# One list of places for all operations of a packed-attention and SoLU kernel, and low parts of w_out made by products

## The chip, the cores and the metric

The kernel runs on one core of a Trainium2 chip. The metric is the device time of one execution in microseconds (us); the time before is the median of three runs. The profile is one further execution on the same kind of chip.

The engines have short names: PE is TensorE (PEld its weight loads), DVE is VectorE, ACT is ScalarE, POOL is GpSimd, and SP is the engine that issues the DMAs. Each engine takes its instructions in program order; between engines, semaphores make one wait for another. The matrix products go to PSUM banks, which are given out from small pools.

## The reference

```
# q, k, v: (8 batches, 8 heads, 576 rows, 64), p: (8, 8, 32, 64), float32; w_in (512, 1024), w_out (1024, 512)
def sm_attn(qq, kk, vv):
    s = scale * np.matmul(qq, kk.transpose(0, 1, 3, 2))
    s = s - np.max(s, axis=-1, keepdims=True)
    a = np.exp(s)
    a = a / (np.sum(a, axis=-1, keepdims=True) + 1e-09)
    return np.matmul(a, vv)
p_packed = sm_attn(p, k, v)
out = sm_attn(q, p_packed, p_packed)
...
h = x @ w_in                      # x: (4608 tokens, 512), the attention's output
h_max = np.max(h, axis=-1, keepdims=True)
e = np.exp(h - h_max)
sm = e / (np.sum(e, axis=-1, keepdims=True) + 1e-09)
solu = h * sm
mu = np.mean(solu, axis=-1, keepdims=True)
var = np.mean((solu - mu) ** 2, axis=-1, keepdims=True)
ln = (solu - mu) / np.sqrt(var + 1e-06) * g_ln
return (ln @ w_out).astype(np.float32)
```

The two weights arrive as 64-bit floats (8 MB together); the kernel itself turns their words into float32.

## The kernel before, in words

Weights. w_in is loaded in four blocks and w_out in four blocks of 1 MB each. To make float32 of a block takes two steps on ACT (lines 534 and 544: the exponent part, then the last bits; block 0 has its last bits done by DVE, LOW_BY = 'daaaaaaa'), one on DVE that joins them (line 545, the magnitude), two products on PE that sum the columns of magnitudes (line 560 or 620), and one on DVE that sets the sign (line 550, signed). Then w_out is scaled by a power of two and by g_ln and split into a high half-precision part wch (ACT, line 636) and a low one wcl = scaled w_out - wch (DVE, line 637); eight chunks of 128x512, so eight steps each.

Attention of a batch b (names as in the tables of the program): lk, lv, lq load k, v, q; kt and qt turn k and q by 32x32 blocks on DVE (batch 0: by products with the identity on PE and copies on ACT); s10, s11 are the scores of the pack queries on PE, mx the maxima on DVE, ex the exponentials on ACT; tp and tc transpose them (PE, ACT); av is the product with v; pp scales its rows (DVE), pt and pc transpose (PE, DVE), pk, to and un make the batch's power-of-two unit. sx0, sx1 are the scores of the second attention (PE), sb puts them into blocks (DVE), sm, su, se, ss, sn are its softmax (DVE, POOL, ACT, DVE, POOL; in batch 0 su and sn are on DVE). z0, z1 multiply the packed rows by w_in (PE), zh and zl are the high and low halves of that (ACT, DVE; in batch 0 POOL makes three of the four zl from copies by ACT, ZL_BY). at, ah, al turn the second attention's weights and split them (DVE, ACT, POOL).

Token tiles. There are 36 tiles of 128 tokens; batch b has 576 tokens, so tiles 4, 13, 22 and 31 lie half in one batch and half in the next. For a tile: m1 is 12 products of 512 columns (attention weights by z, in a high and a low part; line 1173) into an h bank pair, of which there are two; nm is the row maximum and bd a bound (DVE), ex the exponential (ACT, line 1193), u = e * h (DVE, line 1198), which frees h; mu the mean (POOL); yh and yl the high and low half of u - mu (ACT line 1206, DVE line 1209); tr a transposing DMA; m2a and m2b are 24 products by wch and wcl (PE, line 1232) into the one bank po; sq and cr make the row's factor (ACT, POOL); ev writes the tile from po (ACT, line 1236), st stores it. An h pair is free after u, the po bank after ev.

What sets the order. Batch 0 and the weights are written out by hand, with a priority for each step (tables PACK0, W_IN, UNPACK0, W_OUT, PARTS), and the framework's own scheduler places their instructions. Batches 1 to 7 and the tiles are operations of a plan: each has a due place, for example tile number plus a figure for the step,

```
add(i + where[name], f'{name}-{i}', fn, args, needs, takes, gives)
```

and perform() issues the first in that order whose needs are done and whose buffers are free; manual dependencies keep this order on each engine. Thirteen products of ones by ones (keep_busy, line 581) stand at three places to keep PE at work; their results are not used.

Of the kernel before, what the change touches and what calls it, by code (L numbers as in the profile page):

```python
# [19 lines left out]
A_TOP = 15  # L20
LOW_BY = 'daaaaaaa'
ZL_BY = 'ppdp'
A2L_BY = 'pddd'
B0_BY = 'dddd'
PACK0 = [-5, 395, 2010, 10, -1605, 60, -2910, 200, 195]
W_IN = [-50, -50, 4100, 50]
UNPACK0 = [-50, 350, -95, 0, 0, -25, -20, 0, 280]
W_OUT = [-1050, 0, -1030, 2990]
SCALE_AT = 610
CHUNKS = [4, 2, 1, 7, 5, 6, 0, 3]  # L30
PARTS = [100, -2850, 3000, 0, -2010, -1050, -3750, 200]
AHEAD = 0
NPA = 3
NPO = 1
B1_ROWS = 0
TILE = {'m1': -0.05,
 'nm': 0.519,
 'bd': -2.929,
 'ex': 0.729,
 'u': -4.879,  # L40
 'mu': 0.979,
 'yh': 0.948,
 'yl': 1.201,
 'tr': -3.808,
 'sq': 2.299,
 'cr': 0.617,
 'm2a': 2.36,
 'm2b': 2.62,
 'ev': 2.833,
 'st': 3.924,  # L50
 'busy': 0.088}
ATT = {'lk0': -17.433,
 'lk1': -11.934,
 'lk2': -10.358,
 'lk3': -7.951,
 'lv0': -11.338,
 'lv1': -9.338,
 'lv2': -6.267,
 'lq0': -13.937,
 'lq1': -11.104,  # L60
 'lq2': -10.158,
 'lq3': -6.991,
 'kt0': -6.473,
 'kt1': -11.582,
 'kt2': -40.791,
 'kt3': -12.895,
 's10': -5.478,
 'mx0': -29.228,
 'ex0': -4.953,
 'es0': -6.154,  # L70
 's11': -6.498,
 'mx1': -31.812,
 'ex1': -4.556,
 'es1': -5.662,
 'rs': -10.952,
 'tp0': -37.333,
 'tc0': -16.585,
 'tp1': -23.866,
 'tc1': -5.94,
 'tp2': -45.982,  # L80
 'tc2': -30.812,
 'av': -4.062,
 'pp': -36.699,
 'pt': -3.743,
 'pk': -21.304,
 'pc': -3.628,
 'to': -2.366,
 'un': -14.125,
 'qt0': -5.112,
 'qt1': -4.802,  # L90
 'qt2': -6.292,
 'qt3': -26.802,
 'sx0': -12.059,
 'sb0': -2.809,
 'sx1': -32.569,
 'sb1': -19.701,
 'sm0': -27.009,
 'su0': -32.306,
 'se0': -12.207,
 'ss0': -13.505,  # L100
 'sn0': -15.146,
 'sm1': -2.44,
 'su1': -1.798,
 'se1': -13.119,
 'ss1': -17.879,
 'sn1': -9.579,
 'z0': -2.081,
 'zh0': -14.416,
 'zl0': -10.393,
 'z1': -0.678,  # L110
 'zh1': -0.357,
 'zl1': -0.394,
 'at0': -0.887,
 'ah0': -16.535,
 'al0': -2.069,
 'at1': -0.509,
 'ah1': -26.161,
 'al1': -35.456}
MORE = {1: {'lk0': -17.127,
     'lk1': -10.418,  # L120
     'lk2': -9.443,
     'lk3': -8.697,
     'lv0': -9.318,
     'lv1': -57.431,
     'lv2': -5.306,
     'lq0': -13.393,
     'lq1': -9.739,
     'lq2': -6.037,
     'lq3': -5.441,
     'kt0': -6.813,  # L130
     'kt1': -17.476,
     'kt2': -23.913,
     'kt3': -15.876,
     's10': -6.487,
     'mx0': -40.712,
     'ex0': -13.175,
     'es0': -3.538,
     's11': -5.503,
     'mx1': -25.02,
     'ex1': -16.458,  # L140
     'es1': -36.133,
     'rs': -18.456,
# [36 lines left out]
     'zl1': -22.172,
     'at0': -0.926,  # L180
     'ah0': -10.634,
     'al0': -16.855,
     'at1': -6.048,
     'ah1': -32.66,
     'al1': -27.591},
 '1': {'lk0': -31.677,
       'lk1': -21.074,
       'lk2': -14.417,
       'lk3': -10.52,
       'lv0': -29.172,  # L190
# [60 lines left out]
       'al1': -20.563},
 't0': {'m1': -5.97,
        'nm': -10.524,
        'bd': -4.667,
        'ex': -10.568,
        'u': -16.555,
        'mu': -27.616,
        'yh': -22.199,
        'yl': -27.731,
        'tr': -13.33,  # L260
        'sq': -5.133,
        'cr': -7.345,
# [60 lines left out]
        'yl': -1.729,
        'tr': -1.96,
        'sq': -0.595,
        'cr': 0.135,
        'm2a': 2.872,
        'm2b': -13.057,
        'ev': -18.471,
        'st': 1.764,  # L330
        'busy': -0.291},
 't33': {'m1': 0.331,
         'nm': -1.714,
         'bd': -14.347,
# [24 lines left out]
         'm2a': 11.669,
# [29 lines left out]

# [888 lines left out]
```

## Time and profile before

| | |
|---|---|
| median of three runs | 435.77 us (435.16 to 435.9) |
| the profiled execution | 433.67 us, of which its span on the core is 431.9 us |
| PE busy | 388.8 us, 90% of the span |
| DVE busy | 331.3 us, 77% |
| ACT busy | 247.7 us, 57% |
| POOL busy | 135.3 us, 31% |
| moved by DMA | 66.99 MB, mean 155 GB/s |

The profile's page gives the busy time of each engine, the groups of instructions by line, and the chain of work that ended last. A further view gives busy time by stretches ("windows"); the clock in it is the share of TensorE's full clock that was granted. Matrix products overlap their neighbours, so one that is busy for 0.38 us can follow the one before after 0.22 us. Where rows on DVE or ACT follow back to back, one starts up to 0.1 us before the other's recorded end.

### The profile page before, as it was taken

What the parts mean: (1) busy time and instruction counts of PE and PEld (TensorE: products, weight loads), DVE (VectorE), ACT (ScalarE), POOL (GpSimd) and SP (SyncE); (2) the same over time, 40 slices, a digit from 0 to 9 for tenths busy, and PEclk for the clock granted to TensorE, in tenths of its full rate; (3) what the DMA queues carried; (4) which work ended last, traced back from release to release, by engine and by line L of the source; (5) the groups of instructions that cost most, each with busy time, mean ns of one, the idle gap of its engine ahead of it and who ended that gap; (6) DMA issues with size and microseconds to landing.
All of it is one profiled execution on the core that took longest, in us unless ns stands there. A gap on an engine that the chain in (4) does not pass through costs nothing.

```text
span 431.9 us, 8093 instructions
## 1 busy us (share of the span) xinstructions
PE 388.8 (90%) x3053; PEld 179.5 (42%) x3053; DVE 331.3 (77%) x662; ACT 247.7 (57%) x422; POOL 135.3 (31%) x268
## 2 busy tenths in 40 slices
PE   7697075499999999999999999999999999999985
PEld 6472021243443344344543453345434543444432
DVE  3459997769898878897879897988888969765540
ACT  2687453634563686467546844776376636755641
POOL 0000431106332343434115533441153525421230
PEclk9999668699999999999999999999999999999999
DMA  9999970799898957949787969296645431324372
GB/s 272 354 335 258 231 123 15 145 163 180 162 212 180 174 109 184 169 79 190 166 190 146 200 96 257 49 178 151 163 102 114 118 103 45 103 75 121 74 154 66
DMA packets 243383, 66.99 MB, mean 155 GB/s; under 512 B 216464, under 2 KB 236944, under 8 KB 242832
## 3 DMA queue, kind: packets, MB, share of 16 engines
q1 hardware_dynamic: 243344, 66.47, 69.2%
q8 instruction: 24, 0.39, 0.4%
q14 instruction: 15, 0.12, 0.1%
HBM read 37.23 MB, written 9.44 MB: 108 GB/s over the span
## 4 chain that ended last, share of the span: by engine, by line
PE 75%; DVE 10%; ACT 5%; issue 4%; SPq 3%; DMA 2%; POOL 1%; ACTq 0%; DVEq 0%
PE po L1232 41%; PE h L1173 19%; PE pa L1066 4%; PE pa L991 3%; PE pa L940 2%; PE pa L974 2%; PE pa L1028 2%; DVE u L1198 2%; DMA zh<-in_moe_w_in_dram 2%; SPq L449 1%; ACT yhl L1206 1%; DVE yhl L1209 1%; SPq L441 1%; DVE nm L1177 1%; PE pa L581 1%
## 5 line engine op out<-in xcount | busy, mean ns | idle before, releaser
L1232 PE MATMUL po<-wch,yT 128*128 128x512 f16 x576 | 181.8, 380 | 1.9 <-ACT o_sb L1236 1.9
L1232 PEld LDWEIGHTS <-yT 128*128 128x128 f16 x864 | 81.7, 98 | 112.1 <-issue 19.2
L1232 PE MATMUL po<-wcl,yT 128*128 128x512 f16 x288 | 109.2, 379 | 0.0
L1173 PE MATMUL h<-zh,a2h 128*128 128x512 f16 (+1 forms) x160 | 56.4, 391 | 12.1 <-ACT a2h L835 7.8
L1209 DVE SCALAR_TENSOR_TENSOR yhl<-u,negmu,yhl 128x1024 f16<-128x1024 f32 x36 | 45.6, 1265 | 23.7 <-ACT yhl L1206 23.7
L1193 ACT ACTIVATE e<-h,bias,unit 128x1024 f32<-128x1024 f32 x36 | 43.3, 1202 | 34.8 <-DVE bound L1185 21.5
L1198 DVE SCALAR_TENSOR_TENSOR u<-e,s_row,h 128x1024 f32<-128x1024 f32 x36 | 45.9, 1276 | 16.7 <-ACT e L1193 16.3
L1173 PE MATMUL h<-zh,a2l 128*128 128x512 f16 (+1 forms) x160 | 55.9, 387 | 0.3 <-POOL a2l L836 0.3
L1173 PE MATMUL h<-zl,a2h 128*128 128x512 f16 (+1 forms) x160 | 55.9, 387 | 0.0
L1206 ACT ACTIVATE yhl<-u,negmu 128x1024 f16<-128x1024 f32 x36 | 41.3, 1147 | 19.6 <-POOL negmu L1202 19.2
L1173 PEld LDWEIGHTS <-a2h 128*128 128x128 f16 (+1 forms) x320 | 27.9, 102 | 50.7 <-issue 9.6
L1177 DVE TENSOR_REDUCE nm<-h 128x1 f32<-128x1024 f32 x36 | 43.4, 1206 | 1.6 <-PE h L1173 1.6
L1236 ACT ACTIVATE o_sb<-po,c_row 128x512 f32<-128x512 f32 x36 | 24.6, 682 | 34.2 <-PE po L1232 15.3
L1217 ACT ACTIVATE e<-u,negmu 128x1024 f32<-128x1024 f32 x36 | 41.0, 1138 | 0.0
L1202 POOL TENSOR_SCALAR negmu<-su 128x1 f32<-128x1 f32 x36 | 6.8, 190 | 89.0 <-DVE u L1198 84.9
L1224 POOL TENSOR_SCALAR c_row<-sq,k_out,s_eps 128x1 f32<-128x1 f32 x36 | 15.7, 436 | 47.4 <-ACT e L1217 46.0
L1094 POOL TENSOR_TENSOR a2l<-s,a2h 128x576 f16<-128x576 f32 x14 | 18.8, 1343 | 29.4 <-ACT a2h L1090 29.4
L1042 POOL TENSOR_TENSOR s<-s,mx 128x576 f32<-128x576 f32 x14 | 17.2, 1227 | 26.5 <-DVE mx L1039 26.5
L1055 POOL TENSOR_TENSOR a<-a,sm 128x576 f32<-128x576 f32 x14 | 18.6, 1332 | 19.6 <-DVE sm L1052 19.6
L955 ACT ACTIVATE e<-pa,nmx 128x288 f32<-128x288 f32 x28 | 13.7, 494 | 19.1 <-DVE nmx L947 19.1
L1046 ACT ACTIVATE a<-s 128x576 f32<-128x576 f32 x14 | 9.5, 682 | 24.6 <-POOL s L1042 24.6
L1173 PEld LDWEIGHTS <-a2l 128*128 128x128 f16 (+1 forms) x160 | 14.6, 102 | 18.7 <-issue 1.3
(153 smaller groups left out, 544.5 us busy)
## 6 DMA issues: line engine op xcount, KB each, us to landing
out_dram<-o_sb SPq DMA_DIRECT2D x36, 256.0 KB, 2.9
v_sb<-in_v_dram SPq DMA_DIRECT2D x16, 512.0 KB, 5.2
raw<-in_k_dram SPq DMA_DIRECT2D x28, 288.0 KB, 4.7
raw<-in_q_dram SPq DMA_DIRECT2D x28, 288.0 KB, 3.9
zh<-in_moe_w_in_dram SPq DMA_DIRECT2D x2, 1024.0 KB, 5.8
zl<-in_moe_w_in_dram SPq DMA_DIRECT2D x2, 1024.0 KB, 6.8
raw<-in_moe_w_out_dram SPq DMA_DIRECT2D x2, 1024.0 KB, 7.6
zh<-in_moe_w_out_dram SPq DMA_DIRECT2D x2, 1024.0 KB, 8.1
```

Of the source, the lines that this page charges most:

```text
L1055: nc.gpsimd.tensor_tensor(out=st['a2', r], in0=st['a2', r], in1=st['sm', r].unsqueeze(2).broadcast_to([P, NB, J]), op=ALU.mult)
L1066: nc.tensor.matmul(bank[r][32 * g:32 * g + 32, :], lhsT=st['ppT'][rows, r, 32 * g:32 * g + 32], rhs=w_in_sb[rows, g, 512 * n:512 * n + 512 ...
L1094: nc.gpsimd.tensor_tensor(out=lo, in0=a2T, in1=hi, op=ALU.subtract)
L1173: nc.tensor.matmul(h[rows, 512 * n:512 * n + 512], lhsT=lhsT, rhs=z[:, r, 512 * n:512 * n + 512], start=t == 0, stop=t == end)
L1177: nc.vector.tensor_reduce(out=nm, in_=st['h'], axis=AX.X, op=ALU.max, negate=True)
L1193: nc.scalar.activation(st['e'], st['h'], AF.Exp, bias=st['bias'], scale=st['unit'][:, 1:2], accum_out=st['se'])
L1198: nc.vector.scalar_tensor_tensor(out=st['u'], in0=st['e'], scalar=st['s_row'], in1=st['h'], op0=ALU.mult, op1=ALU.mult, accum_out=st['su'])
L1206: nc.scalar.activation(st['y'][:, 0], st['u'], AF.Identity, bias=st['negmu'])
L1209: nc.vector.scalar_tensor_tensor(out=st['y'][:, 1], in0=st['u'], scalar=st['negmu'], in1=st['y'][:, 0], op0=ALU.add, op1=ALU.subtract)
L1217: nc.scalar.activation(st['e'], st['u'], AF.Square, bias=st['negmu'], accum_out=st['sq'])
L1232: nc.tensor.matmul(st['po'], lhsT=st['yT'][:, a, c], rhs=w[:, c], start=c == 0 and t == 0, stop=c == NFC - 1 and t == 2)
L1236: nc.scalar.activation(st['o'], st['po'], AF.Copy, scale=st['c'])
```

## The change

All operations, the loads and the weights' conversion and batch 0 among them, become operations of the plan, and their places come from one list of some 1,500 names. A name is op/batch, op-tile, or op/w for the weights' preparation: lw0 to lw3 load blocks of w_in and lW0 to lW3 blocks of w_out; for the eight blocks wa and wl are the two steps on ACT, wm the magnitude, wp the column sums, ws the sign; ch, cm and cl concern the eight chunks of wch and wcl; lp, p0, lP, pa, pd, px prepare p.

- The token tiles are listed out of turn: 0, 3, 2, 1, 5, 6, 4, 7, 9, 10, 12, 8, 11, 13 and so on by m1; the tiles across two batches come after whole tiles of their second batch.
- The low part of a chunk of w_out is made on PE: a float32 product of a diagonal matrix of the scale (diag, ACT) and w_out, from which a half-precision product of minus the identity and wch is subtracted in PSUM; ACT casts the bank to wcl. DVE has no wcl step left.
- In batch 0 all four zl and both al are DVE's; POOL has no elementwise step there. All eight blocks take their last bits on ACT.
- The keep_busy products are gone (FILL holds zeros).
- v of batch 0 is loaded later, w_in's second block earlier.

```
-LOW_BY = 'daaaaaaa'
-ZL_BY = 'ppdp'
-A2L_BY = 'pddd'
...
+A2L_BY = 'dd'
...
+CL_PE = '11111111'
...
+FILL = [0, 0, 0, 0, 0, 0, 0, 0]
+W_OUT_IN = 'rhrl'
+ORDER = '''
+lw0/w wa0/w wl0/w wm0/w wp0/w lw1/w wa1/w wl1/w lk/0 wm1/w wp1/w lw3/w ws1/w lw2/w wa3/w wl3/w ws0/w ka0/0
...
+zl1/0 al0/0 al1/0 cl5/w cm1/w m1-0 mx0/1 ex0/1 ws7/w es0/1 ch6/w s11/1 m1-3 lq3/1 cl1/w cm6/w qt0/1 nm-0 lv0/1
...
-                nc.vector.scalar_tensor_tensor(out=wcl[:, c], in0=w, scalar=gs[:, c:c + 1], in1=wch[:, c], op0=ALU.mult, op1=ALU.subtract)
...
+    def out_low(c):
+        if c in out_ps:
+            nc.scalar.copy(wcl[:, c], out_ps[c])
+            return
...
+    def out_rest(c):
+        diag = mlp.tile([P, P], F32, name='diag', bufs=2)
+        nc.scalar.activation(diag, ident, AF.Copy, scale=gs[0][:, c:c + 1])
+        bank = out_ps[c] = ps_a.tile([P, 512], F32, name='pa')
+        nc.tensor.matmul(bank, lhsT=diag, rhs=wg[c // 2][:, c % 2 * DM:(c % 2 + 1) * DM], start=True, stop=False)
+        nc.tensor.matmul(bank, lhsT=minus, rhs=wch[:, c], start=False, stop=True)
...
-    work = pack(0)
-    for offset in PACK0:
-        run(work, 1, offset)
-    keep_busy(*BUSY[0])
...
-    prepare_w_out()
...
+    PLACE = {at: n for n, at in enumerate(ORDER.split())}
...
-        plan.append((key, len(plan), at, fn, args, set(after), takes.split(), gives.split()))
...
+        plan.append((PLACE[at], len(plan), at, fn, args, set(after), takes.split(), gives.split()))
...
+    def preparation():
...
+            at(f'wm{n}', magnitude, n, after=[f'wa{n}', f'wl{n}'], gives='u')
...
+            at(f'ws{n}', signed, n, after=[f'~wm{n}', f'~wp{n}'], takes='' if n < 4 else 'y' if n % 2 else 'yT', gives=f'e {held}')
...
+    preparation()
-    for b in range(1, B):
+    for b in range(B):
         attention(b)
```

On SP, the first loads before (zh and zl are also the buffers of weight blocks, o_sb that of p, raw that of k, q and w_out):

```order
L472 DMA zh<-in_moe_w_in_dram 128x2048
L494 DMA o_sb<-in_p_dram 32x4x32 x4
L441 DMA raw<-in_k_dram 128x8x128 x2
L449 DMA raw<-in_k_dram 64x4x64 x2
L441 DMA v_sb<-in_v_dram 128x8x128 x2
L468 DMA v_sb<-in_v_dram 64x8x64
L472 DMA zl<-in_moe_w_in_dram 128x2048
L441 DMA raw<-in_q_dram 128x8x128 x2
```

and in the changed kernel, up to the same v:

```order
L215 DMA zl<-in_moe_w_in_dram 128x2048
L215 DMA zh<-in_moe_w_in_dram 128x2048
L189 DMA o_sb<-in_p_dram 32x4x32 x4
L215 DMA zh<-in_moe_w_out_dram 128x2x1024
L127 DMA raw<-in_q_dram 128x8x128 x2
L135 DMA raw<-in_q_dram 64x4x64 x2
L202 DMA g_sb<-in_moe_g_ln_dram 128x8x1
L215 DMA raw<-in_moe_w_out_dram 128x2x1024 x2
L127 DMA v_sb<-in_v_dram 128x8x128 x2
```

Two more blocks of w_in and k stand ahead of these rows. v has moved from behind k to behind q and three blocks of w_out.

On DVE, the rows from the end of batch 0's softmax to the first row maximum of a token tile (nm), before:

```order
L830 STREAM_TRANSPOSE s_529<-a_484 128x576
L630 TENSOR_SCALAR gs<-g_sb,w_scale 128x8
L836 TENSOR_TENSOR a2l_179<-s_529,a2h_178 128x576
L637 SCALAR_TENSOR_TENSOR wcl<-yhl,gs,wch 128x512 x2
L637 SCALAR_TENSOR_TENSOR wcl<-yT,gs,wch 128x512
L637 SCALAR_TENSOR_TENSOR wcl<-yhl,gs,wch 128x512
L637 SCALAR_TENSOR_TENSOR wcl<-yT,gs,wch 128x512 x3
L637 SCALAR_TENSOR_TENSOR wcl<-yhl,gs,wch 128x512
L1177 TENSOR_REDUCE nm<-h 128x1
```

and now:

```order
L618 STREAM_TRANSPOSE s_596<-a_550 128x576
L428 STREAM_TRANSPOSE kT<-raw 128x576
L614 SCALAR_TENSOR_TENSOR zl<-h,unit,zh 128x512 x2
L633 TENSOR_TENSOR a2l_107<-s_558,a2h_106 128x576
L633 TENSOR_TENSOR a2l_107<-s_596,a2h_106 128x576
L456 TENSOR_REDUCE mx_641<-pa 128x1 x2
L458 TENSOR_REDUCE nmx<-mx_641 128x1
L256 SCALAR_TENSOR_TENSOR yhl<-zl,e 128x1024
L474 TENSOR_REDUCE ssum<-es 128x1
L428 STREAM_TRANSPOSE qT<-raw 128x576
L725 TENSOR_REDUCE nm<-h 128x1
```

The eight wcl are gone, two al (a2l) stand where one stood, and k, scores and q of batch 1 (kT, mx, qT) have moved ahead of the first nm.

On PE, the rows around the first m1 (its first products are those with a2h) in the changed kernel:

```order
L451 MATMUL pa<-kT,pT_84 32x288 x8
L342 MATMUL pa<-yT,diag 128x512
L343 LDWEIGHTS minus
L343 MATMUL pa<-wch,minus 128x512
L721 LDWEIGHTS a2h_106
L721 MATMUL h<-zh,a2h_106 128x512
```

and before:

```order
L620 LDWEIGHTS mag
L620 MATMUL po<-e,mag 128x512
L1173 LDWEIGHTS a2h_178
L1173 MATMUL h<-zh,a2h_178 128x512
L1173 LDWEIGHTS a2h_178
L1173 MATMUL h<-zl,a2h_178 128x512
```

The scores s10 of batch 1 and the products for a chunk of wcl now stand ahead of the first m1; before, three m1 stood there and batch 1's scores came behind them.

More of the change, by code (lines that the diff above doesn't have):

```diff
@@ L52 @@
[L52 to L118, printed above, removed]
@@ L559, in convert_in, with signed @@
         for i in range(2):
-            nc.tensor.matmul(w_sums[0], lhsT=ones_b, rhs=upper(bits, i), start=g + i == 0, stop=g == G - 1 and i == 1)
-        signed(w_in_sb[:, g], bits, w_in_raw[g])
-        if g == G - 1:
-            nc.vector.tensor_reduce(out=w_bound, in_=w_sums[0], axis=AX.X, op=ALU.max)
+            nc.tensor.matmul(sums[m], lhsT=g_abs[0][:, 2 * (n - 4) + i] if m else ones_b, rhs=upper(bits_of[n], i), start=n % 4 + i == 0, stop=n % 4 == 3 and i == 1)
+    def signed(n):
+        if n < 4:
+            dst = w_in_sb[:, n]
+        else:
+            dst = wg[n - 4] = mlp.tile([P, 2 * DF], F16, name='yhl' if n % 2 else 'yT', bufs=2).bitcast(F32)
+        nc.vector.scalar_tensor_tensor(out=dst.bitcast(I32), in0=words_of(w_raw[n])[1], scalar=-2147483648, in1=bits_of[n], op0=ALU.bitwise_and, op1=ALU.bitwise_or)
@@ L864, in perform, with add @@
+    def add(at, fn, args, after=(), takes='', gives=''):
+        plan.append((PLACE[at], len(plan), at, fn, args, set(after), takes.split(), gives.split()))
     def perform():
@@ L1061, in z_mm @@
                 st['z'] = (zh[b % 2], zl[b % 2])
-            bank = st['zp', n] = [ps_a.tile([P, 512], F32, name='pa') for _ in range(2)]
+            bank = st['zp', n] = banks(2)
             for g in range(G):
@@ new lines, in attention @@
+        two = 'pa pa' if b else 'h'
+        for name, ready in (('k', ['s10', 's11']), ('q', [])):
+            T = name + 'T'
+            for g in range(G):
+                if b < ROWS:
+                    wide = name in IN_H[b]
+                    at(f'{name}a{g}', transpose_rows, st, T, name, g, wide, after=[f'l{name}'] + [f'~{name}a{g - 1}'] * (g > 0), takes='h' if wide else 'pa' if g else 'pa pa', gives='raw' * (g == 3))
+                    at(f'{name}c{g}', copy_rows, st, T, g, wide, after=[f'{name}a{g}'] + [f'~{name}c{g - 1}'] * (g > 0), takes='' if g else T, gives='h' if wide else 'pa' if g < 3 else 'pa pa')
+                else:
+                    at(f'{name}t{g}', turn, T, name, g, after=[f'l{name}{c}' for c in range(4)] + ['~s11-1' if name == 'k' else '~sx1-1'] if g == 0 else [f'~{name}t{g - 1}'], takes='' if g else T, gives='raw' if g == 3 else '')
@@ L1106, in attention @@
+        kT, qT, v_in = (['kt3'], ['qt3'], ['lv0', 'lv1', 'lv2']) if b >= ROWS else ([f'kc{g}' for g in range(G)] + ['=p0/w'] * (b == 0), [f'qc{g}' for g in range(G)], ['lv'])
         for r in range(2):
-            at(f's1{r}', s1, r, after=['kt3', '~tp2-1'] + ['s10'] * r, takes='pa pa', gives='kT' * r)
+            at(f's1{r}', s1 if b >= ROWS else s1_first, r, after=kT + ['~tp2-1'] + ['~s10'] * r + ['=px/w'] * (b == 1), takes=two, gives='kT' * r)
             at(f'mx{r}', s1_max, r, after=[f's1{r}'])
-            at(f'ex{r}', s1_exp, r, after=[f'mx{r}'] + ['ex0'] * r, takes='' if r else 'e1', gives='pa pa')
@@ L1117, in attention @@
+        at('pe', row_peak, after=['pp'])
         at('pt', pp_turn, after=['pp'], takes='pa')
         at('pc', pp_copy, after=['pt'], takes='ppT')
-        at('pk', peak_sum, after=['pp', '~pc'], gives='pp')
+        at('pk', peak_sum, after=['pe', 'pc'], gives='pp')
         at('to', peak_copy, after=['pk', '~pc'], gives='pa')
-        at('un', scale, after=['to'])
-        if rows_first:
-            at('qt3', turn_rows, after=['lq3'], takes='qT h h', gives='raw h h')
-        else:
-            for g in range(G):
-                at(f'qt{g}', turn, 'qT', 'q', g, after=['lq3'] if g == 0 else [f'qt{g - 1}'], takes='' if g else 'qT', gives='raw' if g == 3 else '')
```

993 lines of the change are left out of this document (311 added, 682 removed).

## The prediction

> **What bounds the kernel now.** I read the page's first line, then the windows, then the chain of waits and the waits of the early stretch, to see in which stretches TensorE (PE) is short of work or of clock.
>
> ```profile
> span 431.9 us, 8093 instructions
> ...
> 0.00:10.00 10.00, 7.24 (x46) 6.49 (x48) 3.60 (x7) 2.61 (x3) 0.90 (x8) 1.00 0.91 266
> 10.00:20.00 10.00, 6.47 (x89) 4.38 (x86) 3.86 (x9) 6.64 (x17) 0.00 (x0) 0.99 1.11 343
> 20.00:30.00 10.00, 10.00 (x159) 7.07 (x157) 4.58 (x8) 8.08 (x15) 0.00 (x0) 0.84 1.02 385
> 30.00:40.00 10.00, 8.50 (x78) 3.94 (x74) 9.71 (x16) 8.32 (x12) 0.00 (x0) 1.00 0.99 278
> 40.00:50.00 10.00, 3.08 (x28) 0.58 (x20) 10.00 (x13) 6.46 (x9) 4.57 (x4) 0.86 1.00 201
> 50.00:60.00 10.00, 3.67 (x9) 1.14 (x10) 9.89 (x20) 5.19 (x9) 4.53 (x5) 0.50 1.10 203
> ...
> 60.00:104.50 44.50, 31.93 (x267) 13.86 (x266) 33.97 (x71) 20.99 (x38) 10.11 (x21) 0.84 0.62 118
> 104.50:410.00 305.50, 301.83 (x2330) 135.15 (x2329) 251.19 (x517) 182.96 (x313) 111.63 (x222) 1.00 0.66 139
> 410.00:431.90 21.90, 16.04 (x73) 6.94 (x71) 4.51 (x8) 6.47 (x10) 3.57 (x10) 1.00 0.45 109
> ```
>
> A windows row gives its length, then the busy time of PE, weight loads, VectorE (DVE), ScalarE (ACT) and GpSimd, the granted clock, the DMA share and GB/s. From 104.5 to 410 PE is busy 301.83 of 305.5 us at full clock: only 3.7 us can be had there. Ahead of that, DMA is full until 60, DVE is full from 30 to 60 (9.71, 10.00, 9.89), and from 60 to 104.5 PE is busy 31.93 of 44.5 at a clock of 0.84. So the change can win at the start, nearly nowhere else.
>
> What each unit of PE work costs at full clock is read from the chain of waits (start, us, what):
>
> ```profile
> 91.80 1.02 PE pa L1066 x16
> ...
> 195.94 0.65 PE pa L940 x16
> ...
> 205.65 1.16 PE pa L974 x10
> ...
> 209.40 1.66 PE pa L991 x80
> ...
> 402.40 5.18 PE po L1232 x24
> 407.58 2.60 PE h L1173 x12
> ```
>
> A token tile is 2.6 (m1) and 5.2 (m2); the attention of one batch is two s1 (0.65), the transposes (1.16), av (1.66), two sx (of s1's shape), two z (1.02) and about 0.5 of small pieces: 8.0.
>
> By 104.5 the kernel before has done three m1, batch 1's attention and two tiles' m2: 7.8 + 8.0 + 10.4 = 26.2 us of work. With 301.8 and 16.0 the token phase holds 344 us of PE work, and it begins at 57.4 with the first m1. Of the 47.1 us from there to 104.5 some 21 are lost. The waits of 57 to 105 and PE's own rows say how:
>
> ```profile
> PE pa L974 <- ACT e L955: 4.8, 1, 4.8
> PE h L1173 <- DVE u L1198: 4.4, 1, 4.4
> PE pa L940 <- ACT e L955: 2.5, 1, 2.5
> ...
> 58.20 0.63 PE L1173 MATMUL h<-zl,a2h 128*128 128x512 f16 x1
> 58.62 0.63 PE L1173 MATMUL h<-zh,a2l 128*128 128x512 f16 x1
> ...
> 61.22 0.38 PE L1173 MATMUL h<-zh,a2h 128*128 128x512 f16 x1
> 61.44 0.38 PE L1173 MATMUL h<-zl,a2h 128*128 128x512 f16 x1
> ```
>
> 11.7 us are waits for the softmax of batch 1 and for a tile's u. Matmuls follow each other after 0.42 us at 58 and after 0.22 at 61: behind an idle stretch PE runs at half speed for some us.
>
> **The change, part by part.** The prices on DVE, GpSimd (POOL) and ACT:
>
> ```profile
> 30.26 0.61 DVE L718 TENSOR_SCALAR pp<-pa,rs 128x128 f32<-128x128 f32 x2
> ...
> 41.33 1.21 DVE L545 SCALAR_TENSOR_TENSOR e<-e,u 128x1024 int32<-128x1024 int32 x1
> 43.18 0.74 DVE L775 TENSOR_TENSOR s<-s,mx 128x576 f32<-128x576 f32 x1
> 43.84 1.22 DVE L550 SCALAR_TENSOR_TENSOR yT<-raw,e 128x1024 int32<-128x1024 int32 x1
> 44.98 2.18 DVE L545 SCALAR_TENSOR_TENSOR e<-e,u 128x1024 int32<-128x1024 int32 x1
> 47.08 1.71 DVE L775 TENSOR_TENSOR s<-s,mx 128x576 f32<-128x576 f32 x1
> ...
> 58.13 1.42 DVE L637 SCALAR_TENSOR_TENSOR wcl<-yhl,gs,wch 128x512 f16<-128x512 f32 x2
> 62.79 0.74 DVE L637 SCALAR_TENSOR_TENSOR wcl<-yhl,gs,wch 128x512 f16<-128x512 f32 x1
> 64.01 1.22 DVE L1177 TENSOR_REDUCE nm<-h 128x1 f32<-128x1024 f32 x1 [0.49 <-PE h L1173]
> 70.97 2.75 DVE L926 STREAM_TRANSPOSE kT<-raw 128x576 f32<-128x576 f32 x4
> 79.45 1.28 DVE L1209 SCALAR_TENSOR_TENSOR yhl<-u,negmu,yhl 128x1024 f16<-128x1024 f32 x1 [1.50 <-ACT yhl L1206]
> ...
> 44.06 4.11 POOL L824 TENSOR_TENSOR zl<-o_sb,zh 128x512 f16<-128x512 f32 x2 [1.17 <-ACT o_sb L823]
> ...
> 31.01 1.16 ACT L534 ACTIVATE e<-raw 128x1024 f32<-128x1024 f32 x1
> 42.72 0.69 ACT L820 ACTIVATE zh<-h,unit 128x512 f16<-128x512 f32 x1
> ```
>
> 1. The loads. In the new list v stands behind four blocks of w_in, k, p, one block of w_out, q and two more of w_out: 11 MB with v itself. At 266, 343 and 385 GB/s the first 30 us move 9.9 MB, so v lands at about 33. The queue's in-order waits are short: the first block of w_out waits for w_in block 0's signed (by ACT's and DVE's rows about 14.5, while loads up to 18 are still under way), the third for k's transposes (about 22). av takes about 2 us behind v; the conversion of w_out's third block stands ahead of pp on DVE, behind 2 x 1.1 on ACT. So pp starts at about 36, where before it is 30.3: 6 us late.
>
> 2. From pp to the first m1. Before, 30.3 to 57.4, 27.1 us with DVE full. On that stretch the new list has three magnitude steps (wm) and four signed steps (ws) of w_out fewer (7 x 1.15, since steps back to back follow each other some 0.06 before their duration is over: the eight wcl take 58.13 to 63.53, 0.68 each). It no longer has POOL beside it: with POOL's zl running at 44.06 to 48.2 a DVE step takes 1.71 for 0.74, and 2.18 for 1.21; that is about 2.8 over three steps (the third, L782, is of the same form as L775). It gains batch 1's kT (2.75), three zl and one al (0.68 each, 2.7). Sum: 27.1 - 8.0 - 2.8 + 5.5 = 21.8; adding the new rows one by one gives 23.2. I take 23.5: the first m1 at 59.5 to 60, not at 57.4.
>
> 3. Low parts of w_out. Eight wcl (5.4 us) leave DVE. ACT gets eight casts from PSUM (bound: 0.69 of L820, 0.57 back to back), eight diag steps of 128x128 (between nothing and the 0.69 of four times the width) and one conversion step more (1.16): 5.7 to 12 us, of which I take 8 since the diag is small, less three copies for POOL (2.1). PE gets eight float32 products 128x512 and eight f16 ones. The nearest float32 rows: sixteen 64x512 products, eight side by side, in 1.02, so 0.51 each pass of the array; with 0.22 for the f16 one 0.73, in all 5.8 us (twice that as the upper bound). Six of the eight lie ahead of the first m1, where PE is busy 3.1 and 3.7 of 10 us and ACT 6.5 and 5.2: hidden. If ACT were full there, the last cast and diag ahead of the first m1 would move it; by its rows ACT is through at 58. Two lie behind it: +1.4.
>
> 4. From the first m1 on. Between the last al and the end of the first yl DVE has two nm (1.22), one signed (1.22), four qT (2.75, as kT), u and yl (1.28 each, of one shape), pp (0.61) and some 4 us of maxima, bounds and sums: 13.6. So the first yl ends at 73.2 (before 80.7), its transpose lands 3.9 later:
>
> ```profile
> yT<-yhl SPq DMA_TRANSPOSE x36, 3.9
> ```
>
> Meanwhile PE has four m1, since the tiles 0, 3, 2, 1 all belong to batch 0 and the list holds tile 4 back, plus s11, transposes, av, sx0 and z0 of batch 1 (s10 is done). Each wait of before has cover: u of tile 0 comes while PE does tile 3's m1. I followed rows and durations to the first m2 at 79.6 (before 87.8) and to m1 of tile 5 at 96.0; by then 32.7 us of the token phase are done: the four m1, three tiles' m2 but half of one, batch 1's attention, batch 2's s1. Before reaches 26.2 at 104.5. That is (104.5 - 96.0) + (32.7 - 26.2) = 15 us ahead.
>
> 5. The middle has 3.7 us to win and new waits to lose; DVE has 251 of 305 us there, so the list need not be perfect. I cost it at nothing, between -3 and +14 (seven batches, 2 each).
>
> 6. The end. Four m2 follow each other with one po bank, before three; each pays for o_sb:
>
> ```profile
> 422.63 0.38 PE L1232 MATMUL po<-wch,yT 128*128 128x512 f16 x1 [0.78 <-ACT o_sb L1236]
> ```
>
> +0.8. The dummies (13 products) fall in idle PE time: nothing, if the clock holds.
>
> **Sum.** 431.9 - 15 + 0.8, and 1 to 2 for what a walk by hand forgets: 419, or 13 less. The other way round: 60 + 344 - 0.7 (s10 done) + 1.4 + 3.5 (idle and half speed behind the first m1) + 3.7 + 5.9 (the end without PE) + 0.8 = 418.6. The profiled execution lasted 433.67 and the median of the runs is 435.77, so a median of 435.8 - 13 = 423. Differences under 0.2% (0.9 us) are what a measurement of this kernel can't tell from none.
>
> **Rivals.** (a) The start gives nothing: v, sixth in the queue, or ACT, which carries all conversions and the casts, moves the first m1 to 70. For it: ACT is busy 8 of 10 us from 20 to 40 already. Against: 10 us more than its rows sum to. Time: 433. (b) Slower: PE stays at half speed. The dummies are gone, and PE is thinly used from 42 to 60; 16 us of PE work lie between the first m1 and the first m2. At half speed all of it adds 16: 423 + 16 = 439. It decides from 13 us on. For it: clock 0.50 at 50 to 60 and 0.84 to 104.5. Against: the row at 61.22 has full speed 5 us behind the start, and the new list has no wait over 3 us there. The Trainium skill, "TensorE: Matmul & The Clock Gate", part 1, says that a window of about 3.4 us without work halves the clock, and one of sustained work restores it; the trace agrees (0.42 to 0.22 within 5 us). By that rule the loss would be one window, some 2 us, as the sum has it. (c) The middle gets new waits, through the load queue:
>
> ```profile
> SPq L1213 <- DVE yhl L1209: 123.6, 29, 10.8
> ```
>
> SP takes its issues in turn and stands 123.6 us behind transposes that wait for yl; in the new list the loads of k and q of two batches are mixed in between. If a k lands late, s1 holds PE: seven batches, 2 us each, +14: 437 at worst, no change at 13. Against: PE waits hardly at all though SP waits so long before, and DVE has 18% of slack. (d) The middle also gets rid of its waits and the walk loses nothing: 423 - 5 = 418, down to 413.
>
> **How the numbers follow.** Forecast 0.53 (416 to 430), (d) 0.18, (a) 0.11, (c) 0.10, (b) 0.08. Faster: 0.53 + 0.18 + 0.11 + 0.03 of (c) = 0.85; same 0.04; slower 0.03 of (c) and 0.08 of (b) = 0.11. The range 411 to 433 leaves out (b), most of (c) and the far end of (a) and (d).
>
> **What would show it.** Right: first m1 at 58 to 62; four m1 within 20 us of it; first m2 at 78 to 83; DVE over 9 of 10 from 60 to 100; no wcl on DVE; DVE's subtractions at 0.74 while batch 0 runs; PE over 98% from 105 on. Wrong: first m1 behind 66, a clock under 0.9 behind 65, or PE waits of over 10 us in the middle.

## The result and the profile after

The changed kernel takes 419.33 us (median of four runs, 417.3 to 420.75), beside 435.47 us for the kernel before on the same chip (four runs, 432.92 to 435.9): ratio 0.963, 95% interval 0.961 to 0.966. The forecast was 423 (411 to 433). The profiled execution lasted 420.75 us, its span is 418.9; the sum on record for it was 419.

The windows of the changed kernel, in the columns explained for before:

```profile
span 418.9 us, 8114 instructions
...
40.00:50.00 10.00, 6.12 (x40) 1.87 (x26) 9.55 (x23) 6.97 (x13) 1.02 (x4) 0.83 1.03 164
50.00:60.00 10.00, 6.11 (x29) 2.04 (x28) 9.06 (x14) 6.72 (x14) 0.00 (x0) 0.98 0.97 200
60.00:104.50 44.50, 42.97 (x354) 19.32 (x353) 40.85 (x92) 29.83 (x60) 15.22 (x26) 0.97 0.78 156
104.50:397.00 292.50, 286.64 (x2241) 127.84 (x2240) 245.33 (x494) 174.90 (x296) 112.55 (x217) 1.00 0.68 141
397.00:418.90 21.90, 16.02 (x72) 6.94 (x71) 2.54 (x4) 5.75 (x9) 4.20 (x9) 0.98 0.47 109
```

PE is busy 42.97 of the 44.5 us from 60 to 104.5, where it was busy 31.93. From 104.5 on it has 286.64 + 16.02 = 302.7 us of work left; before it had 301.83 + 16.04 = 317.9. So at 104.5 the changed kernel is 15.2 us of PE work ahead. It gives 2.2 back in the middle, where PE is idle 5.9 us and before 3.7; the last 21.9 us hold the same work in both. 15.2 - 2.2 = 13.0, the difference of the spans.

The steps at the start, from the timeline (start, us, engine, what, and in brackets the idle time ahead and who ended it):

```profile
35.88 0.60 DVE L514 TENSOR_SCALAR pp<-pa,rs 128x128 f32<-128x128 f32 x2
...
45.52 0.76 DVE L566 TENSOR_TENSOR s<-s,mx 128x576 f32<-128x576 f32 x1
...
50.20 1.02 PE L342 MATMUL pa<-yhl,diag 128*128 128x512 f32 x2
51.06 0.38 PE L343 MATMUL pa<-wch,minus 128*128 128x512 f16 x1
53.48 1.13 PE L342 MATMUL pa<-yT,diag 128*128 128x512 f32 x2 [2.04 <-ACT diag L340]
...
58.59 0.41 ACT L340 ACTIVATE diag<-ident,gs 128x128 f32<-128x128 f32 x1
58.90 1.42 DVE L633 TENSOR_TENSOR a2l<-s,a2h 128x576 f16<-128x576 f32 x2
59.06 1.53 PE L342 MATMUL pa<-yT,diag 128*128 128x512 f32 x2
60.81 0.64 PE L721 MATMUL h<-zh,a2h 128*128 128x512 f16 x1
61.23 0.63 PE L721 MATMUL h<-zl,a2h 128*128 128x512 f16 x1
64.71 1.23 DVE L725 TENSOR_REDUCE nm<-h 128x1 f32<-128x1024 f32 x1 [1.32 <-PE h L721]
73.22 1.28 DVE L757 SCALAR_TENSOR_TENSOR yhl<-u,negmu,yhl 128x1024 f16<-128x1024 f32 x1
80.94 0.39 PE L780 MATMUL po<-wch,yT 128*128 128x512 f16 x1
```

pp starts at 35.9 (about 36 on record), the first m1 at 60.8 (59.5 to 60), the first m2 at 80.9 (79.6). A chunk's float32 product takes 0.86 us from its start to that of the product behind it (50.20 to 51.06), not 0.51. The first m1 begins with PE at half speed: products 0.42 apart at 60.81 and 61.23, and nm waits 1.32 for them.

The first yl, the first transposes and the first m2 of the kernel before, and then the first transpose of the changed kernel:

```profile
69.77 1.28 DVE L1209 SCALAR_TENSOR_TENSOR yhl<-u,negmu,yhl 128x1024 f16<-128x1024 f32 x1 [1.50 <-ACT yhl L1206]
80.76 3.65 SPq L1213 DMA_TRANSPOSE yT<-yhl  x2
87.77 0.55 PE L1232 MATMUL po<-wch,yT 128*128 128x512 f16 x1
```

```profile
74.56 1.68 SPq L761 DMA_TRANSPOSE yT<-yhl  x1
```

So the first yl ends 3.5 us later than before (74.50 for 71.05), and the first m2 nevertheless starts 6.8 us earlier. Before, the first two transposes were issued only from 80.76 on, and PE did batch 1's transposes and av ahead of the first m2; now the transpose follows its yl at once.

The waits of PE on po behind 104.5, and the SP queue's longest:

```profile
PE po L780 <- DMA yT<-yhl: 4.0, 4, 1.5
PE po L780 <- ACT o_sb L784: 1.1, 3, 0.8
...
SPq L761 <- DVE yhl L757: 82.6, 22, 8.4
```

### The profile page after: what moved, and what is told of

Read it like the earlier page. It is cut to its first block, busy times and chain, and to the rows that moved or that the text cites. A ratio compares the mean times of both kernels' runs of the same rounds, so it can differ in the third digit from the quotient of the medians.

```text
span 418.9 us, 8114 instructions
## 1 busy us (share of the span) xinstructions
PE 385.6 (92%) x3064; PEld 177.2 (42%) x3064; DVE 330.2 (79%) x657; ACT 252.6 (60%) x437; POOL 133.9 (32%) x264
## 4 chain that ended last, share of the span: by engine, by line
PE 65%; DMA 8%; ACT 8%; DVE 7%; SPq 5%; issue 3%; POOL 2%; ACTq 0%; DVEq 0%; POOLq 0%
PE po L780 37%; PE h L721 18%; DMA yT<-yhl 4%; SPq L135 2%; SPq L412 2%; PE pa L590 2%; DMA zh<-in_moe_w_in_dram 2%; ACT o_sb L784 2%; PE pa L554 2%; PE pa L488 1%; DMA raw<-in_moe_w_out_dram 1%; DVE u L746 1%; ACT e L741 1%; PE pa L505 1%; DMA raw<-in_k_dram 1%
## 5 line engine op out<-in xcount | busy, mean ns | idle before, releaser
L780 PE MATMUL po<-wch,yT 128*128 128x512 f16 x576 | 179.4, 380 | 8.0 <-ACT o_sb L784 4.0
L721 PE MATMUL h<-zh,a2h 128*128 128x512 f16 (+1 forms) x160 | 55.4, 384 | 0.0
L757 DVE SCALAR_TENSOR_TENSOR yhl<-u,negmu,yhl 128x1024 f16<-128x1024 f32 x36 | 49.4, 1372 | 7.4 <-ACT yhl L754 6.5
L721 PE MATMUL h<-zh,a2l 128*128 128x512 f16 (+1 forms) x160 | 55.0, 381 | 0.0
L750 POOL TENSOR_SCALAR negmu<-su 128x1 f32<-128x1 f32 x36 | 9.7, 271 | 104.7 <-DVE u L746 72.9
L772 POOL TENSOR_SCALAR c_row<-sq,k_out,s_eps 128x1 f32<-128x1 f32 x36 | 15.2, 423 | 43.1 <-ACT e L765 40.3
L579 POOL TENSOR_TENSOR a<-a,sm 128x576 f32<-128x576 f32 x14 | 17.1, 1220 | 22.6 <-DVE sm L576 17.9
L633 POOL TENSOR_TENSOR a2l<-s,a2h 128x576 f16<-128x576 f32 x14 | 18.3, 1318 | 11.8 <-ACT a2h L629 11.7
L773 POOL TENSOR_TENSOR c_row<-c_row,neg_half 128x1 f32<-128x1 f32 x36 | 21.0, 583 | 3.0
```

Of the source, the lines that this page charges most:

```text
L633: (nc.gpsimd if b or A2L_BY[r] == 'p' else nc.vector).tensor_tensor(out=lo, in0=a2T, in1=hi, op=ALU.subtract)
L721: nc.tensor.matmul(h[rows, 512 * n:512 * n + 512], lhsT=lhsT, rhs=z[:, r, 512 * n:512 * n + 512], start=t == 0, stop=t == end)
L757: nc.vector.scalar_tensor_tensor(out=st['y'][:, 1], in0=st['u'], scalar=st['negmu'], in1=st['y'][:, 0], op0=ALU.add, op1=ALU.subtract)
L773: nc.gpsimd.tensor_tensor(out=c_row, in0=c_row, in1=neg_half, op=ALU.pow)
L780: nc.tensor.matmul(st['po'], lhsT=st['yT'][:, a, c], rhs=w[:, c], start=c == 0 and t == 0, stop=c == NFC - 1 and t == 2)
```

## The experiments

"Changed" is the kernel above, 418.9 us of span in its first profile. Each ratio is to the kernel before, run on the same chip; for the changed kernel it is 0.963.

**1. Low parts back on VectorE.**

```
-CL_PE = '11111111'
+CL_PE = '00000000'
```

> All eight low parts of w_out are subtracted on VectorE again, at the places where the list has the casts; all else as changed. My theory, that VectorE sets the pace from pp to the first yl: eight steps of 0.68 us come back to it, five of them ahead of the first m1. The first m1 goes from 60.8 to about 63.7, the first yl from 74.5 to about 79, the first m2 from 80.9 to about 85, and the time rises by 3 to 5 us, to 422.5 to 424.5 (ratio to the kernel before 0.970 to 0.975). The rival, that the eight products of 1.07 us on TensorE and the casts on ScalarE cost as much as the steps saved: no difference or up to 2 us less.

Measured: 425.35 us, ratio 0.978 (0.976 to 0.980), span 423.9.

```profile
60.00:104.50 44.50, 39.56 (x325) 16.91 (x326) 42.04 (x89) 24.15 (x46) 15.81 (x25) 0.91 0.83 159
...
55.60 2.43 PE L451 MATMUL pa<-kT,pT 64*32 64x288 f32 x12 [11.30 <-DMA pT<-p2t]
...
61.77 1.41 DVE L633 TENSOR_TENSOR a2l<-s,a2h 128x576 f16<-128x576 f32 x2
63.11 0.74 DVE L336 SCALAR_TENSOR_TENSOR wcl<-yT,gs,wch 128x512 f16<-128x512 f32 x1
67.40 1.18 DVE L725 TENSOR_REDUCE nm<-h 128x1 f32<-128x1024 f32 x1
76.31 1.28 DVE L757 SCALAR_TENSOR_TENSOR yhl<-u,negmu,yhl 128x1024 f16<-128x1024 f32 x1
79.59 0.75 DVE L336 SCALAR_TENSOR_TENSOR wcl<-yhl,gs,wch 128x512 f16<-128x512 f32 x1
```

The al are 2.9 us later than in the changed kernel (61.77 for 58.90), nm 2.7, the first yl 3.1; two wcl more stand behind it. The direction is my theory's, the size was too low: 5.0 us of span and 6.0 of median, expected 3 to 5. The rival, that the products cost as much as they save, is out. One thing was not in the expectation: without the products ahead of batch 1's s10, PE has no work for 11.3 us there, and the clock granted from 60 to 104.5 is 0.91, not 0.97. By an estimate that is 0.06 x 44.5 = 2.7 us of full speed. The 3.1 us up to the first yl are VectorE's steps; how much of the rest is the clock's, this run does not tell.

**2. Batch 1's attention behind the first tile.**

```
-... cm2/w kt0/1 zl0/0 ch3/w ... kt3/1 s10/1 zl1/0 ... yl-0 tr-0 bd-3 pc/1 ...
+... cm2/w zl0/0 ch3/w ... zl1/0 ... yl-0 tr-0 kt0/1 kt1/1 kt2/1 kt3/1 s10/1 mx0/1 ex0/1 ... pp/1 pt/1 bd-3 ...
```

> What the list does for batch 1 between its transposes and the first yT (kT, qT, first product, softmax, exponent) stands behind the transpose of the first token tile; loads and tokens as changed. My theory, that the gain is the attention of batch 1 drawn into the stretch in which PE would be idle: without the four kT steps (2.75 us) the first m1 comes some 3 us earlier, at about 58, and the first m2 at 73 to 76, but PE then stands for some 10 us for batch 1 after the four m1, and the time rises by 5 to 8 us (ratio 0.975 to 0.982). The rival, that the gain is the low parts and the copies alone and the place of batch 1 is no matter: no difference within 1 us, or up to 2 less.

Measured: 432.51 us, ratio 0.996 (0.993 to 0.998), span 430.1.

```profile
60.00:104.50 44.50, 34.59 (x282) 15.01 (x281) 31.52 (x66) 20.40 (x39) 9.67 (x18) 0.88 0.56 116
...
67.61 1.28 DVE L759 SCALAR_TENSOR_TENSOR yhl<-u,negmu,yhl 128x1024 f16<-128x1024 f32 x1
77.80 1.69 PE L453 MATMUL pa<-kT,pT 64*32 64x288 f32 x16 [5.50 <-ACT e L471]
86.95 0.61 DVE L516 TENSOR_SCALAR pp<-pa,rs 128x128 f32<-128x128 f32 x2 [4.61 <-PE pa L507]
```

Nearly the whole gain goes. The first yl is 5.6 us earlier (67.61 for 73.22), but then batch 1's chain of scores, softmax and transposes runs by itself: PE waits 5.5 for the exponentials, DVE 4.6 for PE, and PE's work from 60 to 104.5 falls by 8.4 us. The clock of that stretch falls too, from 0.97 to 0.88: s1 takes 1.69 there and 0.72 in the changed kernel (at 64.61). My expectation had the direction and about half the size (5 to 8, measured 11 of span and 13 of median). One thing limits what this run shows: the list keeps the first m2 behind batch 1's z0, so it starts at 93.04 although its transpose was issued at 68.96. A list that also draws m2 into the waits was not run, so the 11 us are the price of this one place and not of every order with batch 1 late.

**3. Token tiles in turn.**

```
-... m1-0 ... m1-3 ... m1-2 ... m1-1 ... m1-5 ... m1-6 ... m1-4 ...
+... m1-0 ... m1-1 ... m1-2 ... m1-3 ... m1-4 ... m1-5 ... m1-6 ...
```

> The same list with the token tiles renamed, so that tile k stands at the kth place; nothing else differs. My theory, that four tiles of batch 0 come first in both and that the tile that straddles two batches finds both ready at the fifth place: no difference, -1.5 to +1.5 us, first m2 at 80 to 82. The rival, that the order out of turn is what lets the token phase run without waits: fifth m1 some 3 us later and the same at each further straddling tile, 3 to 10 us slower.

Measured: 418.44 us, ratio 0.963 (0.961 to 0.965), span 417.4. No difference that can be told, so the order out of turn does nothing by itself. Four tiles of batch 0 come first either way. Its trace has the first m1 at full speed, 0.22 apart (61.27 and 61.49). The list that is renamed here has 1168 names, not some 1,500.

**4. v early.**

```
-lw0/w ... wl1/w lk/0 wm1/w ... ws4/w lv/0 tc2/0 ...
+lw0/w ... wl1/w lk/0 lv/0 wm1/w ... ws4/w tc2/0 ...
```

> The load of batch 0's v stands right behind that of its k, three loads of the queue earlier than changed (w_in's blocks and the rest follow it). My theory, that until 40 VectorE and the conversions of weights set the pace: w_in's later blocks land some 3 us later, and the time is the same or up to 3 us more; pp between 35 and 38. The rival, that the landing of v holds pp: pp 2 to 5 us earlier, the first m1 as well, 2 to 4 us less in all.

Measured: 422.84 us, ratio 0.973 (0.971 to 0.975), span 422.2. ACT's conversion of w_in's third block, of the changed kernel and then of this one, and the pp and nm of this one:

```profile
14.77 1.14 ACT L230 ACTIVATE e<-zl 128x1024 f32<-128x1024 f32 x1 [4.16 <-DMA zl<-in_moe_w_in_dram]
```

```profile
18.56 1.12 ACT L232 ACTIVATE e<-zl 128x1024 f32<-128x1024 f32 x1 [8.26 <-DMA zl<-in_moe_w_in_dram]
...
42.42 0.60 DVE L516 TENSOR_SCALAR pp<-pa,rs 128x128 f32<-128x128 f32 x2
...
68.82 1.19 DVE L727 TENSOR_REDUCE nm<-h 128x1 f32<-128x1024 f32 x1
```

The conversion starts 3.8 us later, pp 6.5 (42.42 for 35.88, outside my 35 to 38), nm 4.1 and the end 3.3. So an earlier v does not help: it delays the blocks of w_in, and that moves pp. In the changed kernel's trace av starts at 33.54 behind PE's own transposes of q, without idle time ahead of it, so v does not hold it there. v's late place is better than this early one, though pp itself comes later than in the kernel before.

**5. The last two chunks on VectorE.**

```
-CL_PE = '11111111'
+CL_PE = '11111100'
```

> Only the low parts of chunks 6 and 7, whose products stand behind the first m1, go back to VectorE: TensorE loses 2 x 1.07 us, ScalarE two casts and two diag steps (1.9 us), VectorE gets 2 x 0.68. My theory, after the first experiment (eight steps back cost 5 us of span, five of them ahead of the first m1): behind the first m1 both engines are nearly full, so it changes by less than 1 us; were TensorE alone the bound there, 1 to 2 us less; were VectorE alone the bound, 1.4 us more.

Measured: 420.62 us, ratio 0.966 (0.963 to 0.969), span 418.8. The intervals overlap: no verdict between "no change" and "1.4 us more". One to two us less is out, so the two products behind the first m1 are not what bounds that stretch.

**6. Both undone** (edits 1 and 2 together).

> The first two experiments together: low parts on VectorE, and batch 1's attention behind the transpose of the first token tile. Each alone cost 5.0 and 11.2 us of span against the changed kernel (418.9). My theory, that these two hold the whole gain and what is left of the change (loads, no POOL copies, the middle) comes out near nothing: 430 to 436 us of span, the kernel before having 431.9. The rival, that the rest of the change gains several us by itself: 424 to 428, and then the two effects overlap.

Measured: 432.59 us, ratio 0.995 (0.993 to 0.998), span 429.4. The first yl, PE's wait for kT, and nm of the fourth tile; then that nm in experiment 2:

```profile
69.29 1.28 DVE L759 SCALAR_TENSOR_TENSOR yhl<-u,negmu,yhl 128x1024 f16<-128x1024 f32 x1
71.32 3.15 PE L453 MATMUL pa<-kT,pT 64*32 64x288 f32 x18 [5.23 <-DVE kT L430]
108.05 1.21 DVE L727 TENSOR_REDUCE nm<-h 128x1 f32<-128x1024 f32 x1
```

```profile
108.20 1.22 DVE L727 TENSOR_REDUCE nm<-h 128x1 f32<-128x1024 f32 x1
```

The effects don't add: 5.0 and 11.2 us of span alone, 10.5 together. Where batch 1 comes late, low parts on PE are worth nothing (432.51 with them, 432.59 without; the first yl is 1.7 us later without, and by the fourth tile that is gone). Where batch 1 is drawn ahead they are worth 5 us of span. The likely reason is that kT, qT and batch 1's softmax then want the same DVE, which is busy 42.04 of the 44.5 us from 60 to 104.5 in experiment 1 and 35.58 here; no run separates this from the clock. What is left of the change, its loads, no POOL copies and the middle, is worth 2.5 us of span (429.4 for 431.9) and 2.6 of median (432.59 for 435.15). The span is just below the 430 that my theory set as its lower end: the two parts hold most of the gain, as the theory says, but they overlap, as the rival says.

**7. Three zl by GpSimd again.**

```
+ZL_BY = 'ppdp'
...
+                if b == 0 and ZL_BY[2 * n + r] == 'p':
+                    st['zc', n, r] = mlp.tile([P, 512], F32, name='o_sb', bufs=2)
+                    nc.scalar.activation(st['zc', n, r], st['zp', n][r], AF.Copy, scale=units[b][:, 0:1])
...
+                    nc.gpsimd.tensor_tensor(out=st['z'][1][:, r, cols], in0=st['zc', n, r], in1=st['z'][0][:, r, cols], op=ALU.subtract)
```

> Three of the four low parts of batch 0's z are made as in the kernel before: a copy on ScalarE and a subtraction on GpSimd, in place of one step on VectorE each. VectorE is relieved of 3 x 0.68 = 2.0 us, GpSimd gets 3 x 2.05. My theory, that work of GpSimd stretches VectorE's steps beside it (1.71 for 0.74 in the kernel before): VectorE's steps at 51 to 60 take twice as long, which gives back 2 to 4 us; ScalarE gets 1.7 us more; the first m1 0 to 2 us later and the time 0 to +2 us. The rival, that the long steps of before had another reason: steps stay at 0.74, the first m1 and the time 1 to 2 us earlier.

Measured: 418.54 us, ratio 0.963 (0.959 to 0.966), span 415.8: no difference in the runs.

```profile
45.00 2.79 POOL L616 TENSOR_TENSOR zl<-o_sb,zh 128x512 f16<-128x512 f32 x2
45.13 1.64 DVE L567 TENSOR_TENSOR s<-s,mx 128x576 f32<-128x576 f32 x1
...
51.85 2.06 DVE L429 STREAM_TRANSPOSE kT<-raw 128x576 f32<-128x576 f32 x3
52.67 1.16 POOL L616 TENSOR_TENSOR zl<-o_sb,zh 128x512 f16<-128x512 f32 x1 [4.88 <-ACT o_sb L610]
```

The stretching is real (1.64 for 0.76), but it meets a few steps alone: three transposes beside POOL's third step take the usual 0.69 each. DVE gives back about 1 us here and saves 2, so that taking the copies away was no gain in itself; my guess of 2 to 4 us given back was too high. The first m1 starts at 59.66, 1.2 us earlier than in the changed kernel's first profile, and nm at 62.45, 2.3 earlier. That is the rival's sense and not my theory's (0 to 2 later), but no gain in time follows from it.

**8. Dummies ahead of the first m1.**

```
-FILL = [0, 0, 0, 0, 0, 0, 0, 0]
+FILL = [10, 6, 0, 0, 0, 0, 0, 0]
...
-        spare = ps_a.tile([P, 512], F32, name='pa')
+        spare = ps_o.tile([P, DM], F32, name='po')
...
-                at(f'f{n}', keep_busy, m, takes='pa', gives='pa')
+                at(f'f{n}', keep_busy, m, takes='po', gives='po')
```

with f0 ahead of cm4 and f1 ahead of s10/1 in the list.

> Dummies in idle time of TensorE: ten products ahead of the first low-part product (44.0 to 46.5 is idle) and six ahead of batch 1's first product (an idle 1.8 us stands there); they go to the bank po, which nobody needs there. My theory, that in the changed kernel's profile TensorE ran at half speed from 59 to 62 (matmuls 0.43 apart) because of the idle times ahead of it and that this varies between executions: the first m1 at full speed, span 417 to 418, the median of the times 0.5 to 1.5 us lower. The rival, that dummies come in the way of the products behind them: 0 to +1.5 us.

Measured: 419.42 us, ratio 0.964 (0.961 to 0.966): no gain. Its profiled execution is left out: it lasted 2188 us, with 1.7 us for each half-precision product of 512 columns, a slowness that no other run here has and that stays unexplained. The four others lasted 419.3 to 419.9. Whether the dummies kept the clock up at the first m1 can therefore not be read; the mean granted clock of the four, 0.979 to 0.984, is within the 0.975 to 0.987 of the changed kernel's eight executions.

**9 and 10. Two more steps of batch 0 by GpSimd; the same with tiles in turn.**

```
-A2L_BY = 'dd'
+A2L_BY = 'pd'
...
-            (nc.gpsimd if b else nc.vector).tensor_tensor(out=st['a2', r], ...
+            (nc.gpsimd if b or r == 0 else nc.vector).tensor_tensor(out=st['a2', r], ...
```

> The seventh experiment (three of the four low parts of batch 0's z by GpSimd), and two steps more of batch 0 by GpSimd: the first normalisation of the second softmax and the first low part of a2 (0.76 and 0.68 us of VectorE). In the seventh, GpSimd's subtraction stretched only VectorE's subtraction of two float32 tiles (1.64 for 0.75); transposes beside it kept 0.69. My theory, that VectorE sets the first m1 and is stretched by such steps alone: the first m1 about 2 us earlier than changed (58 to 59 for 60.8), 416.5 to 418 us. The rival, that the chain through GpSimd (its steps take 1.2 to 1.4 us and longer) holds the second softmax and the exponents behind it: no difference or up to 2 us slower.

> The same with the token tiles in turn. My theory, as in the third experiment: no difference from the one with tiles out of turn, within 1 us. The rival: several us slower.

Measured: 419.65 us, ratio 0.966 (0.964 to 0.967), and 418.07 us, ratio 0.963 (0.962 to 0.965); spans 417.9 and 416.3. Neither beats the changed kernel, so the first theory missed, and its rival's "no difference" holds. Tiles in turn come out 1.6 us lower, more than the 1 us that the second theory allowed, but the intervals overlap. DVE waits 1.35 us for POOL's normalisation (its next transpose starts at 49.35), which is the chain that the rival named. Experiment 9:

```profile
49.27 2.27 POOL L616 TENSOR_TENSOR zl<-o_sb,zh 128x512 f16<-128x512 f32 x2
50.80 0.78 DVE L576 TENSOR_SCALAR sm<-sm 128x18 f32<-128x18 f32 x1
54.74 1.28 POOL L640 TENSOR_TENSOR a2l<-s,a2h 128x576 f16<-128x576 f32 x1
54.83 1.80 DVE L580 TENSOR_TENSOR a<-a,sm 128x576 f32<-128x576 f32 x1
...
55.56 1.85 PE L343 MATMUL pa<-yT,diag 128*128 128x512 f32 x2 [1.88 <-ACT diag L341]
...
62.32 0.38 PE L728 MATMUL h<-zh,a2h 128*128 128x512 f16 x1
```

DVE's step starts 0.09 behind POOL's and ends 0.61 behind its end (56.02), nearly its own 0.72: it waits until POOL is through. In this execution PE fell to half speed at 55.56 (1.85 for the 1.12 of experiment 10), the casts behind it came late, and the first m1 starts at 62.32 though its operands on DVE are ready at 59.8. In experiment 10, the same program but for the tiles' numbers, it starts at 59.98.

**11. The changed kernel again.**

> The changed kernel again, nothing edited, beside the two on the same chip. All theories: 418.5 to 420.5 us; its trace shows whether the half speed of TensorE at the first m1 (0.43 between matmuls at 61) comes in each execution: if it is chance, the first m1 may stand at 0.22 here.

Measured: 418.08 us, ratio 0.962 (0.961 to 0.964), span 416.9.

```profile
59.31 1.42 DVE L633 TENSOR_TENSOR a2l<-s,a2h 128x576 f16<-128x576 f32 x2
...
60.65 0.38 PE L721 MATMUL h<-zh,a2h 128*128 128x512 f16 x1
60.86 0.38 PE L721 MATMUL h<-zl,a2h 128*128 128x512 f16 x1
...
63.73 1.19 DVE L725 TENSOR_REDUCE nm<-h 128x1 f32<-128x1024 f32 x1
```

The same program has its first m1 at full speed here. al is 0.4 later than in the first profile, nm nevertheless 1.0 earlier, the end 2.0 earlier. So half speed at that place is chance, worth about 1.4 us (the 0.4 and the 1.0), and differences of that size between the experiments' single profiles say nothing.

## Why the prediction was right, point by point

- Start. Right: pp at 36, a first m1 a few us later than before, the first yl within 1.3 us (it ends at 74.5, 73.2 on record). The step's reason for the late pp, that av waits for v, is not what the trace shows: av starts without a wait, and in experiment 4, with v early, it is w_in's later blocks that delay pp. Two times of the kernel before were misread. Its first m1 starts at 56.02; 57.4 is that tile's third product, behind a short wait for al. And 80.7 is the end of its second yl; the first ends at 71.05. So the forecast of an earlier first yl is wrong in sign, and the first m2 comes earlier for another reason: before, PE did batch 1's attention ahead of it with 11.7 us of waits, now with 0.2. The sum uses neither time, as it goes by the work done at 104.5.
- Low parts. Right in kind: DVE is the engine that counts up to the first yl (3.1 us there), and the eight products in place of the steps are worth 5 us of span in all, a part of which may be PE's clock (experiment 1). The term for PE was mis-sized, 1.07 us a chunk and not 0.73, because a row of 64x512 products was read as one pass of a float32 product; it lay inside the bound of twice the price. Two chunks behind the first m1 are 2.1 us, not 1.4, and experiment 5 shows that they don't bound. A diag step takes 0.41 and a cast 0.57, which makes ACT's part 8 x 0.98 + 1.16 = 9.0, 8 on record, in both before the 2.1 of the copies for POOL comes off.
- POOL. The stretch of DVE's steps is what the trace of before showed, and it is gone (0.76 at 45.52). On record the stretch was 2.8 us gained and the three zl that come to DVE 2.0 lost. Experiment 7 undoes both and gives back about 1 us of stretch for the 2 that it saves, so in this list the two together are no gain.
- From the first m1 to 104.5. The step that carries the result: 15 us ahead on record, 15.2 measured. Experiment 2 shows the main reason, batch 1's attention in the stretch that was empty; experiments 1, 2 and 6 together show that the low parts pay only beside it. That they do so by making room on DVE is read from DVE's rows and not shown apart. In its rows the walk was a little early: m1 of tile 5 starts at 98.63, 96.0 on record.
- Middle. On record nothing; 2.2 us more idle time in the first profile; of the 5.9 us that PE is idle there, 4.0 are waits for yT. Rival (c), loads that come late to s1, shows nowhere: none of PE's waits there is for a load. Rival (d), a middle without its waits, is not what happened either, though the time of 419 lies near its 418.
- End. +0.8 on record; the last 21.9 us of both kernels hold 16.0 us of PE work, so it is nothing.
- Rival (b), a PE that stays slow: full speed from 63 on, clock 0.97. The loss of some 2 us on record is 1.4, in some executions. The Trainium skill, "TensorE: Matmul & The Clock Gate", part 1, adds that the window that it watches runs freely, so that the same kernel starts slow for another number of products each time; the two traces of the changed kernel agree, one at 0.42 and one at 0.22. Half speed came behind an idle time of 1.78 us in the first profile (ahead of 58.27) and of 1.88 in experiment 9, but not behind 2.04 in the first profile (ahead of 53.48).
- From the span to the median. The sum gave 419 and the span is 418.9; 423 came out because the difference to the profiled execution of before was taken off the median of the runs. The changed kernel's first profile was the longest of its four executions (half speed at the first m1; 416.9 in the other profile), and the profile of before was 2.1 us shorter than the median of its runs, so the runs differ by 16 us and the profiles by 13. That the sum hit the span to 0.1 us is luck in part: the 0.8 of the end and the 1 to 2 for what a walk forgets are not there, the middle's 2.2 stands in their place, and the spans of the changed kernel's eight executions run from 415.2 to 418.9.
- Signs on record. Those that were to show it right came, but one: first m1 at 60.8, the fourth m1 through at 79.9, first m2 at 80.9, DVE busy 36.5 of the 40 us from 60 to 100, no wcl on DVE, subtractions at 0.76. PE over 98% from 105 on is just missed (286.14 of 292.0 us up to 397, and 16.02 of the last 21.9). Of those that were to show it wrong none came.

Open: what an order with batch 1 late but m2 drawn ahead would cost, how much of experiment 1's loss is PE's clock, which of the loads, the POOL copies and the middle makes the 2.5 us that are left with both main parts undone, and what the dummies do to the clock.

## What to carry to other kernels

Work that is taken off an engine is worth something only if other work is ready to take its place: here the low parts of w_out gain 5 us of span beside a second batch drawn ahead and nothing without it, so such changes are priced together. To price an order, count the bound engine's work done by a fixed time, before and after; one sum over the windows gave 15.2 us where many rows gave 15. And where the bound engine's clock depends on the idle time ahead, take two profiles of the same program before reading 1 or 2 us out of one.

## What was not expected of the hardware

GpSimd's elementwise step holds up VectorE's subtraction of two float32 tiles (1.64 for 0.76, experiment 7) and their product (1.80 for 0.72, experiment 9), and a small step with one tensor operand too (0.78 for 0.18: it starts at 50.80 and ends at 51.58, POOL's pair of steps at 51.54), but not VectorE's transposes (0.69 each beside it). The Trainium skill, "SBUF — State Buffer", section "SBUF: two separate sides", says that the two engines share a pair of ports as a lock held for a whole instruction, and that it concerns VectorE's steps with two SBUF inputs or in a two-port mode. The first two rows agree with a lock rather than a shared rate: 54.83 ends 0.61 behind POOL's end. For the transposes, the rows agree with their not needing the pair.
